# Opening of a linear-attention and gated-unit kernel: batch 0's second half of values and batch 1's edge planes issued later, batch 2's q and k ahead of the weights

## The chip, the cores and the metric

The kernel runs on one core of a Trainium2 chip. The metric is device time in microseconds (us) of one execution, smaller is better. The engines are TensorE (PE; PEld is its weight load), VectorE (DVE), ScalarE (ACT), GpSimd (POOL) and SyncE (SP, which only issues transfers and passes semaphores on). Transfers between device memory and the on-chip buffer (SBUF) are carried out by 16 DMA engines. GpSimd issues on queue q0, SyncE on q1, ScalarE on q10.

## What is computed

Hedgehog linear attention over 8 batches, 8 heads, 576 tokens, head dimension 64, followed by a causal gated linear unit. All inputs and the output are float32.

```python
def phi(x):
    proj = np.einsum('bhsd,df->bhsf', x, w_phi)              # 64 -> 128 features
    proj = proj - np.max(np.abs(proj), axis=-1, keepdims=True)
    return np.concatenate([np.exp(proj), np.exp(-proj)], axis=-1)
q_p, k_p = phi(q), phi(k)
kv  = np.einsum('bhsf,bhsd->bhfd', k_p, v);  z = np.sum(k_p, axis=2)
num = np.einsum('bhsf,bhfd->bhsd', q_p, kv)
den = np.einsum('bhsf,bhf->bhs', q_p, z)[..., None] + 1e-06
attn = num / den                                             # -> x: [8, 576, 512]
# second part, d_model 512
gate_pre[:, s] = sum over k of conv_w[k] * x[:, s - 4 + k]    # 5 causal taps
gate = 1 / (1 + exp(-gate_pre))
out  = (gate * (x @ w_val)) @ w_out
```

## The kernel before

Each batch is cut into 4 units, one for each pair of heads, and one smaller "edge" part. With x running over 128 partitions, a pair of heads has 9 token planes for each partition. Eight of them are worked on unit by unit, 32 units in all (0 to 3 are batch 0, 4 to 7 batch 1, and so on); the ninth plane of all four units of a batch together is the edge part (names that end in e, numbered by batch).

The order of all work is written out by hand in one string, `ORDER`, of some 1250 tokens. A token is an operation, the number of its unit or batch, after @ its PSUM banks, and after a colon the engine (P GpSimd, D VectorE, A ScalarE). The loop at the end calls `op_<name>` for each token in turn. Each engine runs its own instructions strictly in that order and waits at semaphores for the others. Where two tokens stand on different engines, their relative place in the string says nothing; where they share an engine or an issuing queue, it is the order.

The tokens that matter here, with the lines under which the profile shows them:

- Loads on GpSimd's queue (they turn float32 into bfloat16): `LQa LKa LKb LQb` are batch 0's q and k in pieces, `LQ1 LK1` and `LQ2 LK2` all of batch 1's and 2's (L287, tiles qN, kN); `LWV0` is w_val (L324, tile GV), `LWO0..3` quarters of w_out (L333, tile WOUT).
- Loads on SyncE's queue: `LVa` and `LVb` are the first and second half (two units each) of a batch's values, two transfers each (L292, tile vN); `LE` is its edge plane of values, two transfers in runs of 256 bytes (L297, tile vE).
- `T` transposes q and k of a unit on TensorE (L347), `Te` those of an edge (L637); `Tc` and `Tce` copy the result to SBUF (L154). `PK` and `PQA` project k and q to the features (L360), `mKa mKb mQ` take the maxima on VectorE (L377), `E` and `Ee` their exponentials (L426), `Ka Kb` the exponentials of k on ScalarE (L441), `KTe` those of the edge.
- `V` scales a unit's values on GpSimd (L467, L471; V0 and V1 read what LVa0 loads, V2 and V3 what LVb0 loads, V4 and V5 LVa1), `Ve` the edge's (Ve1 reads LE1). `KV` multiplies them with the k features (L488, L496).
- `PQa`, `PQb` project q a second time, transposed (L534), `DMQ` spreads the maxima on GpSimd (L412), `SH` subtracts them (L550), `Qp Qm` are the exponentials of q (L564).
- `WC` copies w_val, in a permuted layout, to tile WVAL on GpSimd (L154); the gated unit reads it from L839 on, and WOUT from L868 on. `TH` is the gate's tanh (L828).
- `WQ` is a relay: an empty instruction on SyncE (L526) that waits for the last matmul of `PQa`; the first matmul of `PQb` waits for the relay. SyncE's queue thus has transfers and relays in one order.

Lines of the loads and of the relay:

```python
def vload(b, j):
    vs = v[b].rearrange("h (p n) d -> p h (n d)", n=NPL)
    for a in range(2):
        nc.sync.dma_start(vals(b, j)[row(a), :, :], vs[:, 4 * j:4 * j + 4, 4 * a * D:(4 * a + 5) * D])
def op_LE(b):
    for g in range(2):
        e = 8 * D * (1 - g)
        nc.sync.dma_start(plane8(b)[:, g::2, :], src["v"][b, :, g::2, e:e + D])
def relay(u):
    u.relay = nc.sync.nop()
    behind(u.relay, u.last)
```

The buffers for q and k hold three batches, those for values four halves, those for edge planes two batches; so none of the loads of batches 0 to 2 named above waits for a buffer.

Of the kernel before, what the change touches and what calls it, by code (L numbers as in the profile page):

```python
# [20 lines left out]
P = 128  # L21
HP = H // 2
NPL = 9
E1 = D + 1
# [3 lines left out]
ORDER = """  # L28
ZV2:D ZV0:D IF0:D CQ0 CK0 LQa0 FL9@1 ND0:D ZV1:D LKa0 FL7@3 TP0@5 FL2@1 T0@2 CW0 W0 T1@1 Tc0:D PQA0@3 Tc1:A
mQ0 PK0@5,0 Ka0 PK1@6,7 mKb0 Kb1 FL1@2 LKb0 mKa1 LQb0 PQA1@1 mQ1 T2@3 mKa0 Te0@4 Tce0:D FL14@1 Kb0 Tc2:A  # L30
PQA2@0 PK2@4,5 LQ1 LK1 DG0:P LWV0 mKb1 Ka1 E0 E1 LWO0 LK2 LQ2 LE0 LVa0 PQa1@2 DMQ1:P LVb0 LE1 WQ1 DMQ0:P Kb2
V1:P mQ2 DMQ2:P Ka2 PKe0@6 mKe0 mKb2 PQb1 SH1 Ee0 KTe0 LWO1 T3@0 FL5@1 Tc3:D FL11@1 FL12@1 mKa2 FL13@1 Qm1 Qp1
PQa0@0 WQ0 PQb0 SH0 mQe0 PQa2@6 PQA3@4 WQ2 Qm0 PQb2 mQ3 DMQe0:P Ve0:P SH2 Qp0 Qp2 LWO3 V0:P T4@3 Tc4:D T6@2
PQA4@4 Qm2 LWO2 Tc6:D mQ4 DMQ4:P DMQ3:P Te1@3 PK4@1,2 Tce1:D mKa4 KV1@0 KVM1:D PQea0@4 LVa1 WQe0 Kb4 PKe1@6
# [988 lines left out]
```

## Time and profile before

| | |
|---|---|
| Three runs | 219.36, 221.36, 221.43 us; median 221.36 |
| The profiled execution | 220.76 us, of which 219.0 are the span from the first to the last instruction of the profile |
| Mean granted TensorE clock | 0.981 of full speed |
| Moved by the DMA engines | 32.40 MB, mean 148 GB/s |

A row of the timeline or of the chain begins with its start and its length in us, counted from the start of the span; then come engine, line, operation, tiles (out<-in), shapes, the number of instructions that were merged, and in brackets the idle time of that engine just before and what ended it. A row of waits reads "who <- for whom: us in total, times, longest". A row of issues ends with KB of each and median us from issue to landing. A queue row is packets, MB and the time of its packets as a share of 16 engines' time; with two queues at once such shares can add to more than 100%. A row of a stretch has its length, each engine's busy time and number of instructions, the granted clock, the DMA share and GB/s. SPq, POOLq are the issuing sides of these engines.

### The profile page before, as it was taken

To read this page: it belongs to the slowest core of one execution; us is meant where nothing else is said; L and a number is where in the kernel's file an instruction comes from. 1 tells how busy PE (TensorE), PEld (TensorE's weight loads), DVE (VectorE), ACT (ScalarE), POOL (GpSimd) and SP (SyncE) were. 2 spreads that over 40 slices of the span, in tenths; PEclk is the share of its full clock that TensorE was granted. 3 is DMA by queue.
4 is the path that set the end of the run, shared out by engine and by line. 5 is a ranking of instruction groups with operands and counts; after the bars stand their busy time and mean duration, and the time that the engine had idled before them with its cause. 6 is when DMAs were issued, how large, how long until landed. Compare 5 with 4: busy or idle time off the path is not lost.

```text
span 219.0 us, 8941 instructions
## 1 busy us (share of the span) xinstructions
PE 201.0 (92%) x3755; PEld 134.6 (61%) x3788; DVE 188.0 (86%) x339; ACT 193.7 (88%) x386; POOL 149.9 (68%) x180
## 2 busy tenths in 40 slices
PE   7676989979999999999999999999999999999991
PEld 2443758647676676766676668655576667656640
DVE  6786999989999999989989999898998999876362
ACT  3599899998999999999999999799999999988450
POOL 8969968999676498986864768595881695840000
PEclk9969699999999999999999999999999999999998
DMA  6999995069989912999980794719922800404726
GB/s 168 231 256 209 242 218 122 4 136 203 246 183 177 236 34 48 158 226 253 256 201 3 138 196 103 152 31 216 240 49 76 207 15 1 102 18 128 187 57 192
DMA packets 28194, 32.40 MB, mean 148 GB/s; under 512 B 6005, under 2 KB 23285, under 8 KB 28154
## 3 DMA queue, kind: packets, MB, share of 16 engines
q1 hardware_dynamic: 18282, 20.79, 38.7%
q0 software_dynamic: 9328, 10.19, 28.8%
q10 hardware_dynamic: 544, 0.85, 1.2%
q8 instruction: 29, 0.48, 0.9%
q14 instruction: 11, 0.09, 0.2%
HBM read 32.58 MB, written 9.44 MB: 192 GB/s over the span
## 4 chain that ended last, share of the span: by engine, by line
PE 67%; DMA 7%; POOL 6%; issue 5%; DVE 5%; ACT 4%; SPq 3%; POOLq 0%; DVEq 0%; ACTq 0%
PE PS L868 11%; PE PS L839 8%; DMA kN<-in_k_dram 7%; PE PS L496 7%; PE PS L582 6%; PE PS L347 5%; PE PS L360 5%; PE PS L612 4%; PE PS L534 4%; PE PS L796 3%; PE PS L550 3%; PE PS L488 2%; ACT KT L441 2%; PE PS L948 2%; POOL VT L467 2%
## 5 line engine op out<-in xcount | busy, mean ns | idle before, releaser
L467 POOL TENSOR_TENSOR VT<-vN,E 128x1024 bf16<-128x1024 f32 x32 | 61.0, 1905 | 23.3 <-ACT E L426 23.0
L441 ACT ACTIVATE KT<-PS 128x512 bf16<-128x512 f32 x128 | 69.2, 640 | 1.7 <-PE PS L360 0.9
L564 ACT ACTIVATE QT<-PS 128x1024 bf16<-128x1024 f32 x64 | 62.4, 1056 | 1.7 <-PE PS L550 1.4
L377 DVE TENSOR_REDUCE MK<-PS 128x4 f32<-128x512 f32 x64 | 42.6, 682 | 2.9 <-PE PS L360 2.2
L377 DVE TENSOR_REDUCE MQ<-PS 128x8 bf16<-128x1024 f32 x32 | 39.1, 1221 | 4.4 <-PE PS L360 3.8
L412 POOL TENSOR_TENSOR DM<-id,MQ 128x512 bf16<-128x512 bf16 x32 | 33.1, 1040 | 11.7 <-DVE MQ L377 11.4
L868 PE MATMUL PS<-WOUT,GV 128*128 128x512 bf16 x113 | 30.2, 379 | 1.2 <-issue 0.6
L839 PE MATMUL PS<-XT,WVAL 128*128 128x512 bf16 x115 | 29.9, 379 | 0.8 <-issue 0.2
L360 PE MATMUL PS<-W,T 64*128 64x128 bf16 x512 | 24.8, 222 | 2.1 <-ACT T L152 1.1
L496 PE MATMUL PS<-VT,KT 128*128 128x65 bf16 x512 | 24.0, 196 | 0.0
L860 DVE SCALAR_TENSOR_TENSOR GV<-GATE,PS 128x512 bf16<-128x512 bf16 x32 | 21.1, 682 | 3.4 <-ACT GATE L823 2.1
L360 PEld LDWEIGHTS <-T 64*128 64x128 bf16 x512 | 17.6, 97 | 9.1 <-issue 4.0
L602 DVE TENSOR_TENSOR XN<-PS,RCP 128x512 bf16<-128x512 f32 x32 | 21.9, 687 | 0.7
L496 PEld LDWEIGHTS <-KT 128*128 128x128 bf16 x512 | 21.7, 99 | 0.9
L582 PEld LDWEIGHTS <-QT 128*128 128x128 bf16 x512 | 18.4, 97 | 4.8 <-issue 2.4
L582 PE MATMUL PS<-KVS,QT 128*128 128x65 bf16 x512 | 20.8, 193 | 0.0
L534 PE MATMUL PS<-T,W 64*128 64x256 bf16 x128 | 17.8, 281 | 2.5 <-SPq L526 1.2
L154 DVE COPY T<-PS 128x1024 bf16<-128x1024 bf16 x27 | 18.2, 682 | 1.8 <-PE PS L347 1.8
L467 POOL TENSOR_TENSOR VZ<-vE,Ee 64x512 bf16<-64x512 f32 x16 | 16.6, 1039 | 2.9 <-ACT Ee L426 2.3
L839 PEld LDWEIGHTS <-WVAL 128*128 128x128 bf16 x128 | 11.2, 98 | 11.7 <-issue 0.9
L868 PEld LDWEIGHTS <-GV 128*128 128x128 bf16 x128 | 10.8, 98 | 10.8 <-issue 1.3
L488 PE MATMUL PS<-VZ,KTe 128*128 128x130 bf16 x64 | 14.3, 223 | 0.1
(92 smaller groups left out, 365.0 us busy)
## 6 DMA issues: line engine op xcount, KB each, us to landing
vN<-in_v_dram SPq DMA_DIRECT2D x32, 320.0 KB, 7.0
out_dram<-OS SPq DMA_DIRECT2D x28, 256.0 KB, 4.1
qN<-in_q_dram POOLq DMA_DIRECT2D x7, 576.0 KB, 11.4
kN<-in_k_dram POOLq DMA_DIRECT2D x7, 576.0 KB, 10.3
vE<-in_v_dram SPq DMA_DIRECT2D x16, 64.0 KB, 6.4
out_dram<-OSe SPq DMA_DIRECT2D x8, 128.0 KB, 4.8
GV<-in_moe_w_val_dram POOLq DMA_DIRECT2D x1, 512.0 KB, 16.0
WOUT<-in_moe_w_out_dram POOLq DMA_DIRECT2D x4, 128.0 KB, 13.6
```

Of the source, the lines that this page charges most:

```text
L360: (nc.tensor.matmul(PS[:, banks[g], jj * F:(jj + 1) * F], T[row(g), n, jj, :, :].rearrange("p a t -> p (a t)"), W2[row(g), :], start=True, ...
L377: nc.vector.tensor_reduce(dst, x, AX.X, ALU.max, apply_absolute_value=True)
L412: engines[eng].tensor_tensor(u.DM[:, :, :], id64[:, :].unsqueeze(1).to_broadcast([P, n, 64]), u.MQ[:, :, :].rearrange("p j g -> p (j g)"). ...
L441: nc.scalar.activation(u.KT[:, ft, par, :, :].rearrange("p b f -> p (b f)"), PS[:, u.PK[par], :], AF.Exp, scale=1.0 if ft == 0 else -1.0,)
L467: engines[eng].tensor_tensor(dst[:, :, :, 0:D].rearrange("p f (h m) d -> p f h m d", m=m), x.unsqueeze(1).to_broadcast(s), e.rearrange("p ...
L496: nc.tensor.matmul(o, u.KT[:, ft, y % 2, h2 * 2 + y // 2, :], u.VT[:, ft, h2 * 4 + y, :], start=False, stop=(y == 3), skip_group_check=True,)
L534: return nc.tensor.matmul(PS[:, u.PQ + a, :].rearrange("p (j g t) -> p g j t", g=2, t=64)[:, g, :, :], W2[row(g), :], u.T[row(g), 1, :, a, :],
L564: nc.scalar.activation(u.QT[:, ft, :, :, :].rearrange("p a n t -> p a (n t)"), half(u.PQ, 512), AF.Exp, scale=1.0 if ft == 0 else -1.0,)
L582: (nc.tensor.matmul(u.NUM[:, jj // 2, x * E1:(x + 1) * E1], u.QT[:, ft, jj // 2, 4 * h2 + 2 * (jj % 2):4 * h2 + 2 * (jj % 2) + 2, :].rearr ...
L602: nc.vector.tensor_tensor(u.XN[:, :, :, :], numview(u)[:, :, :, 0:D], u.RCP[:, :, :].unsqueeze(3).to_broadcast([P, 2, 4, D]), ALU.mult,)
L839: nc.tensor.matmul(PS[:, m.val[r], :], WVAL[:, dt, r, :], xt(b)[:, dt, 4:12, :].rearrange("p n t -> p (n t)"), start=(dt == 0), stop=(dt = ...
L868: nc.tensor.matmul(PS[:, m.out[j], :], m.GV[:, r, j * P:(j + 1) * P], WOUT[:, r, :], start=(r == 0), stop=(r == 3),)
```

## The change

Only the third line of `ORDER` differs:

```diff
-PQA2@0 PK2@4,5 LQ1 LK1 DG0:P LWV0 mKb1 Ka1 E0 E1 LWO0 LK2 LQ2 LE0 LVa0 PQa1@2 DMQ1:P LVb0 LE1 WQ1 DMQ0:P Kb2
+PQA2@0 PK2@4,5 LQ1 LK1 DG0:P mKb1 Ka1 E0 E1 LK2 LQ2 LWV0 LWO0 LE0 LVa0 PQa1@2 DMQ1:P WQ1 LVb0 LE1 DMQ0:P Kb2
```

On GpSimd's queue `LK2` and `LQ2` are issued ahead of `LWV0` and `LWO0` instead of behind them. On SyncE's queue `LVb0` and `LE1` stand behind the relay `WQ1` instead of ahead of it, so that they are issued after the last matmul of `PQa1`. No instruction is added or removed.

On SyncE (transfers with what each waits for; the relays themselves are not listed, a wait for PE is a relay's), at the second half of batch 0's values:

```order
 L292 DMA vN<-in_v_dram 64x4x320
 L292 DMA vN<-in_v_dram 64x4x320 [waits DMAHW0_49]
-L292 DMA vN<-in_v_dram 64x4x320 [waits DMAHW1_49]
+L292 DMA vN<-in_v_dram 64x4x320 [waits PE_49,DMAHW1_49]
 L292 DMA vN<-in_v_dram 64x4x320 [waits DMAHW2_49]
 L297 DMA vE<-in_v_dram 128x2x64 [waits DMAHW3_49]
```

The first of LVb0's two transfers now waits for TensorE; the rest of the row keeps its order.

On GpSimd, just before the first spreading of q's maxima (kN and qN here are batch 2's k and q, GV is w_val, WOUT the first quarter of w_out):

```order
 L278 TENSOR_TENSOR DIAG<-id_140,cwT 128x640
+L287 DMA kN<-in_k_dram 128x4x576
+L287 DMA qN<-in_q_dram 128x4x576
 L324 DMA GV<-in_moe_w_val_dram 128x4x512
 L333 DMA WOUT<-in_moe_w_out_dram 32x4x512
-L287 DMA kN<-in_k_dram 128x4x576
-L287 DMA qN<-in_q_dram 128x4x576
 L412 TENSOR_TENSOR DM<-id_138,MQ 128x512 x2
```

Batch 2's two loads have moved up past the two loads of weights.

## The prediction

> **What bounds the kernel now.** First the page: the engines' busy shares, and the shares of the chain of work that ended last.
>
> ```profile
> span 219.0 us, 8941 instructions
> PE 201.0 (92%) x3755; PEld 134.6 (61%) x3788; DVE 188.0 (86%) x339; ACT 193.7 (88%) x386; POOL 149.9 (68%) x180
> ...
> PE 67%; DMA 7%; POOL 6%; issue 5%; DVE 5%; ACT 4%; SPq 3%; POOLq 0%; DVEq 0%; ACTq 0%
> ```
>
> Taken over the whole span TensorE is the bound, with ScalarE and VectorE close behind. An average hides the opening, and the chain has 7% (15 us) in DMA. So next I read the chain in order of time over the first 48 us.
>
> ```profile
> 5.19 15.80 DMA kN<-in_k_dram
> 20.99 0.05 issue
> 21.03 0.63 PE PS L347 x8
> ```
>
> The transfer is LK1, batch 1's k: issued at 5.19, landed at 20.99, and then the transposes T4 and T6 (L347) run at once, the eight in 0.63. Third, the table of waits, from 19.5 to 45 us, for ScalarE, VectorE, GpSimd and TensorE.
>
> ```profile
> ACT KT L441 <- PE PS L360: 0.6, 1, 0.6
> ACT KT L441 <- DVE MK L377: 0.5, 1, 0.5
> ACT GATE L828 <- PE PS L796: 0.3, 1, 0.3
> ...
> DVE T L154 <- PE PS L347: 1.2, 1, 1.2
> ...
> POOL VT L467 <- ACT E L426: 1.2, 1, 1.2
> POOL VZ L467 <- ACT Ee L426: 1.1, 1, 1.1
> ...
> PE PS L347 <- DMA kN<-in_k_dram: 1.4, 1, 1.4
> ```
>
> LK1 costs TensorE 1.4 us and, behind it, VectorE 1.2. ScalarE has just three waits in 25 us: two hang on LK1's data, the third is that of the first tanh of batch 0's gate, far behind. GpSimd waits twice, both times for ScalarE. So after LK1 **ScalarE sets the pace**, and the change can be worth no more than what ScalarE waits behind LK1.
>
> **The change: when does LK1 land?** LK1 shares the DMA engines with SP's queue. The queue table over four stretches, in this order: 13 to 16 us, 28 to 30, 30.44 to 32.3, and 12.4 to 20.1.
>
> ```profile
> q0 software_dynamic: 331, 0.37, 70.3%
> q1 hardware_dynamic: 331, 0.40, 44.9%
> ...
> q0 software_dynamic: 354, 0.40, 117.5%
> ...
> q0 software_dynamic: 394, 0.37, 122.3%
> ...
> q0 software_dynamic: 942, 1.04, 78.2%
> ```
>
> q0 is GpSimd's queue, q1 SP's. With both full each moves 331 packets in 3 us, 110 per us, one for one. Alone, q0 moves 354 in 2 us: 177 per us. From 30.44 to 32.3 only q0 moves, although SP issued an LVb1 transfer at 30.44: a new transfer on SP's queue needs about 1.9 us to its first packet.
>
> Before, LVa0, LVb0 and LE1 are issued on SP in one run:
>
> ```profile
> 4.43 2.37 SPq L292 DMA_DIRECT2D vN<-in_v_dram  x3
> 6.84 1.24 SPq L297 DMA_DIRECT2D vE<-in_v_dram  x2
> ...
> vN<-in_v_dram SPq DMA_DIRECT2D x1, 320.0 KB, 9.2
> ```
>
> The 9.2 is that of the one issued at 4.43, LVa0's second piece: it lands at 13.6. How far does a landing trail its last packet? LVb1's second piece was issued at 31.1, and from 36 us on hardly a packet moves:
>
> ```profile
> 31.09 0.61 SPq L292 DMA_DIRECT2D vN<-in_v_dram  x1
> ...
> vN<-in_v_dram SPq DMA_DIRECT2D x1, 320.0 KB, 6.1
> ...
> 36.00:40.00 4.00, 3.96 (x88) 3.23 (x81) 4.00 (x11) 4.00 (x10) 3.99 (x5) 1.00 0.01 1
> ```
>
> (The last row is a stretch; its last two numbers are the DMA share and GB/s.) It landed at 37.2, about 1.2 later. So LVa0's packets end and LVb0's start at about 12.4, and from then on they and LE1's stand against LK1, whose own packets end at about 20.1, 0.9 before its landing. What q0 moved between, 942 packets, is the most that stood before LK1's end. After the change they wait for PQa1:
>
> ```profile
> 14.40 0.42 PE L534 MATMUL PS<-T,W 64*128 64x256 bf16 x2
> ```
>
> PQa1 ends at 14.82, so SP issues LVb0 at about 14.9, and its first packet goes at about 16.8. From 12.4 to 16.8 q0 is alone: 4.4 x 177 = 779 packets of its 942. The other 163 at 110 per us take 1.5 us: 18.3, and 0.9 to the landing gives **19.2 instead of 20.99**. From the other side: a restart after only 1.0 us leaves 322 packets to the shared rate, and 19.7.
>
> **What is late next.** T4 stands in TensorE's row behind SH2, Tc4 in VectorE's behind the maximum of unit 3's q:
>
> ```profile
> 19.27 0.38 PE L550 MATMUL PS<-DM,minus 64*128 64x512 bf16 x2
> ...
> 19.31 1.23 DVE L377 TENSOR_REDUCE MQ<-PS 128x8 bf16<-128x1024 f32 x1 [0.60 <-PE PS L360]
> 21.76 1.29 DVE L154 COPY T<-PS 128x1024 bf16<-128x1024 bf16 x2 [1.22 <-PE PS L347]
> ...
> 17.82 5.65 ACT L564 ACTIVATE QT<-PS 128x1024 bf16<-128x1024 f32 x6
> 24.05 2.18 ACT L441 ACTIVATE KT<-PS 128x512 bf16<-128x512 f32 x4 [0.58 <-PE PS L360]
> ...
> 27.94 1.09 ACT L441 ACTIVATE KT<-PS 128x512 bf16<-128x512 f32 x2 [0.54 <-DVE MK L377]
> ```
>
> SH2 ends at 19.65, so T4 runs then and, with the chain's 0.63, ends at 20.28. VectorE is busy to 20.54, and so Tc4 starts at 20.54 rather than 21.76: 1.22 gained, all of VectorE's wait. ScalarE's block of six q exponentials ends at 23.47 whatever LK1 does. PK4, whose end let ScalarE go at 24.05, comes 1.22 earlier, before 23.47: 0.58 gained. The second wait, at 27.94, ends with VectorE's maximum, which comes 1.22 earlier, at 26.7; ScalarE is then ready at 27.40 - 0.58 = 26.82, so this 0.54 goes too. Together **1.12 us**; then ScalarE has no wait up to that tanh, and GpSimd's two waits behind ScalarE, 1.2 and 1.1, take the shift up as well.
>
> **What the moves cost.** No transfer changes its place among SP's own; LVb0 and LE1 only come behind the relay of PQa1. That relay is not held up; those of PQa0 and PQa2 are now queued behind four issues. The relays of PQa1 and PQa0 passed at 14.9 and 17.7:
>
> ```profile
> L526 SPq EVENT_SEMAPHORE  x2: 17/17/17, 14.9 to 17.7; - x2
> ```
>
> By the issues above (2.37 for three vN is 0.79 each, 1.24 for two vE) the four take 2.8: SP is through at 17.7, when PQa0's relay passed. Cost between 0 and some tenths, and TensorE's wait for LK1 lies behind it; I take **0**.
>
> LVb0 feeds V2 on GpSimd, and the weights the WVAL copies there; the third row is Te2, the first to read batch 2's k:
>
> ```profile
> 26.98 1.90 POOL L467 TENSOR_TENSOR VT<-vN,E 128x1024 bf16<-128x1024 f32 x1
> ...
> 38.56 0.61 POOL L154 COPY WVAL<-GV 128x512 bf16<-128x512 bf16 x1
> ...
> 37.19 0.27 PE L637 MATMUL PS<-ident,kN 128*128 128x128 bf16 x2
> ```
>
> LVb0 is two pieces of 64x4 rows, 512 packets: from 16.8 at 110 per us to 21.5, landed by 23; V2, at 26.98, is held by GpSimd's own row before it. I take 0, with 4 us of cover.
>
> The Trainium skill, page "DMA: Bandwidth & Descriptors", section "Rules for kernel authors", speaks against this edit: issue a transfer early and wait for it late, so that its fixed cost lies under compute. By that rule alone, moving LVb0 ten microseconds later gains nothing, and the sum would be 0 or worse; by V2's row it is the sum below, and the case in which the rule wins is in the second rival.
>
> On GpSimd the same four issues stand before the same DMQ1, so it starts no later. All four stand behind LK1 on one queue, so LK1 does not feel the swap. By 36 us all of the opening's traffic was through (the stretch from 36 to 40, above). Batch 2's k and q, part of it, are first read at 37.19, so landing earlier buys nothing. The weights come later, but the order within the traffic does not change its amount. WVAL is read at 38.56, or 37.4 after the shift: 0, with over 1 us of cover in the worst case.
>
> **Sum:** -1.12, all in ScalarE's waits between 23 and 28 us. Everything later is released by engines, so I let it run to the end. The profiled execution: span 219.0, own time 220.76; it would be 217.9 and 219.65. The runs' median is 221.36, 0.6 above the profiled one, and gives 220.25. I forecast 220.0, between the two.
>
> **The rivals.**
>
> First, more than that: the shift also breaks a later wait. The next place where the chain is on SP is at 45 us:
>
> ```profile
> 45.75 2.04 SPq L297
> ...
> 48.42 0.28 PE L534 MATMUL PS<-T,W 64*128 64x256 bf16 x2 [1.23 <-SPq L526]
> ```
>
> One issue of LE2 there takes 2.04 us instead of 0.6, and TensorE waits 1.23 for the relay behind it. If it falls at a better moment, up to 1.2 more goes: 218.8. Against it: whatever slowed it shifts with it.
>
> Second, less: LK1 lands at 20 or later, or the gain is swallowed by GpSimd, which has no wait between 19.5 and V2's end (the table of waits: both of its waits are later ones).
>
> ```profile
> 32.64 0.22 PE PS L488
> ...
> vN<-in_v_dram SPq DMA_DIRECT2D x1, 320.0 KB, 13.1
> ```
>
> For it: 1.9 us for the restart rests on one case. Against: TensorE reads V2's result, complete at about 28.9, only at 32.64 (KV2, the first row). With half of T4's wait left it is -0.5, and 220.6. If LVb0's second piece took 13.1 us from its issue at 15.6, the longest that an early vN took, V2 would come at 28.7, 1.7 late; GpSimd's first wait (1.2) takes most of that, about 0.4 of the gain is left: 220.7. Nothing gained at all: 221.1.
>
> Third, slower: SP is not through in time. If both LE1 issues take 2.04 as at 45.75, SP is busy to 14.9 + 1.6 + 4.1 = 20.6, and the relay that passed at 17.7 is 2.9 late. TensorE's wait for LK1 takes 1.4 of it; 1.5 is left as loss, 222.6, and more if the relay behind it finds TensorE waiting again. It decides from about 19.1 on. Against it: the five early issues in the rows above took 3.6 us together, 0.72 each.
>
> **How the numbers follow.** Forecast 0.5; more 0.18; less or nothing 0.22; slower 0.10. The three runs lie 2.07 apart, so each case spreads by about 1 around its time; 1% is 2.2 us (219.15 and 223.57), about what a measurement of this kernel tells from no change. Faster by over 1%: 0.12 from the first rival, 0.09 from the forecast's lower edge and 0.02 from the second: 0.23. Slower by over 1%: half of the third, where later relays are late too, 0.05. Within: 0.72. The range runs from the first rival less some spread, 218.4, to the third's near edge, 222.0.
>
> **What would show it.** Right: the row of T4 no longer names kN as what it waited for; Tc4 starts near 20.5; ScalarE has no wait from 17.8 to beyond 40; V2 still starts near 27; the first WVAL copy comes about 1.1 earlier, near 37.4; the granted clock of 0.50 between 24 and 26 us may be gone, which would shorten matmuls there but not the time, since ScalarE sets the pace. Wrong: a wait of V2 for vN, of the WVAL copy for GV, of L534 on SP at 17.8 to 20, or a wait that appears after 40 us and gives the 1.1 back.

## The result, and the profile after

The change makes the kernel faster, by 0.5 to 1.2%. Three measurements on the chip, each beside runs of the kernel before. The ratio is over the executions outside the chip's slower state and is not the quotient of the two medians:

| | runs | median us | before, median us | ratio, 95% interval |
|---|---|---|---|---|
| first | 19 | 218.88 | 220.62 (19 runs) | 0.9946 (0.9924 to 0.9967) |
| second | 6 | 218.42 | 220.62 (23) | 0.9884 (0.9835 to 0.9932) |
| third | 12 | 219.04 | 220.51 (23) | 0.9929 (0.9895 to 0.9962) |

In all three the interval lies below 1. The profiled execution took 219.53 us with a span of 217.7 (before: 220.76 and 219.0). The table of waits of ScalarE in the changed kernel, from 17.5 to 45 us:

```profile
ACT GATE L828 <- PE PS L796: 0.3, 1, 0.3
```

Of before's three waits only that of the first tanh is left. TensorE's largest waits from 17.5 to 22 us:

```profile
PE PS L534 <- DVE MQe L377: 0.6, 1, 0.6
PE PS L360 <- DVE T L154: 0.4, 1, 0.4
PE PS L347 <- ACT QT L564: 0.2, 1, 0.2
```

The 1.4 for kN is gone; what holds L347 now is ScalarE, for 0.2. The issue of LK1 (queue table, KB and us from issue to landing) and SyncE's row:

```profile
kN<-in_k_dram POOLq DMA_DIRECT2D x1, 576.0 KB, 13.9
...
15.06 1.26 SPq L292 DMA_DIRECT2D vN<-in_v_dram  x2
16.36 1.12 SPq L297 DMA_DIRECT2D vE<-in_v_dram  x2
```

LK1 lands 13.9 us after its issue at 5.04, at 18.9, where it took 15.8 before. ScalarE's row, at its six exponentials of q, the two places that waited, and the first tanh:

```profile
18.42 5.68 ACT L564 ACTIVATE QT<-PS 128x1024 bf16<-128x1024 f32 x6
23.84 2.22 ACT L441 ACTIVATE KT<-PS 128x512 bf16<-128x512 f32 x4
...
25.94 1.27 ACT L722 ACTIVATE QTe<-PS 128x512 bf16<-128x512 f32 x2
26.89 1.30 ACT L441 ACTIVATE KT<-PS 128x512 bf16<-128x512 f32 x2
...
40.96 1.94 ACT L828 ACTIVATE GATE<-PS 128x1024 bf16<-128x1024 f32 x2 [0.29 <-PE PS L796]
```

No bracket stands at 23.84 and 26.89, where before had 0.58 and 0.54. The same places of before (the block at 17.82, the exponentials at 24.05 and 27.94 stand in the prediction):

```profile
26.31 1.08 ACT L722 ACTIVATE QTe<-PS 128x512 bf16<-128x512 f32 x2
...
41.79 1.02 ACT L828 ACTIVATE GATE<-PS 128x1024 bf16<-128x1024 f32 x1 [0.28 <-PE PS L796]
```

This cuts both executions into three pieces, which is how all the runs below are compared: the **opening** up to the first exponential of q, the **stretch** from there to the first tanh of the gate, and the **rest**.

| | opening | stretch | rest | span |
|---|---|---|---|---|
| before | 17.82 | 23.97 | 177.2 | 219.0 |
| changed | 18.42 | 22.54 | 176.8 | 217.7 |

The opening is 0.6 longer, the stretch, where the change acts, 1.43 shorter, and the rest 0.4 shorter. Further profiles, below, show how far each of the three moves by chance.

### The profile page after: what moved, and what is told of

It is laid out like the page before. It is cut to its first block, busy times and chain, and to the rows that moved or that the text cites. A ratio compares the mean times of both kernels' runs of the same rounds, so it can differ in the third digit from the quotient of the medians.

```text
span 217.7 us, 8974 instructions
## 1 busy us (share of the span) xinstructions
PE 203.6 (94%) x3788; PEld 134.1 (62%) x3788; DVE 187.7 (86%) x339; ACT 192.9 (89%) x386; POOL 149.6 (69%) x180
## 4 chain that ended last, share of the span: by engine, by line
PE 77%; ACT 13%; DMA 3%; issue 3%; DVE 3%; POOL 1%; POOLq 0%; SPq 0%; ACTq 0%; DVEq 0%
PE PS L868 13%; PE PS L839 12%; PE PS L582 7%; PE PS L496 7%; PE PS L360 6%; ACT KT L441 6%; PE PS L347 6%; PE PS L534 4%; PE PS L796 4%; ACT QT L564 4%; PE PS L612 4%; PE PS L550 3%; DMA kN<-in_k_dram 3%; PE PS L488 2%; PE PS L948 2%
## 5 line engine op out<-in xcount | busy, mean ns | idle before, releaser
L868 PE MATMUL PS<-WOUT,GV 128*128 128x512 bf16 x128 | 32.2, 380 | 0.0
L839 PE MATMUL PS<-XT,WVAL 128*128 128x512 bf16 x128 | 31.3, 379 | 0.0
L496 PEld LDWEIGHTS <-KT 128*128 128x128 bf16 x512 | 21.2, 98 | 1.7 <-issue 0.7
## 6 DMA issues: line engine op xcount, KB each, us to landing
WOUT<-in_moe_w_out_dram POOLq DMA_DIRECT2D x4, 128.0 KB, 15.9
```

The source lines that it names most:

```text
L496: nc.tensor.matmul(o, u.KT[:, ft, y % 2, h2 * 2 + y // 2, :], u.VT[:, ft, h2 * 4 + y, :], start=False, stop=(y == 3), skip_group_check=True,)
L839: nc.tensor.matmul(PS[:, m.val[r], :], WVAL[:, dt, r, :], xt(b)[:, dt, 4:12, :].rearrange("p n t -> p (n t)"), start=(dt == 0), stop=(dt = ...
L868: nc.tensor.matmul(PS[:, m.out[j], :], m.GV[:, r, j * P:(j + 1) * P], WOUT[:, r, :], start=(r == 0), stop=(r == 3),)
```

## The experiments

The theory at this point, called A in the expectations: SyncE's part is all of the change; it lets LK1 land earlier, and ScalarE loses its waits behind LK1. Rival B: batch 2's q and k ahead of the weights carry a share. Rival C: the difference between the two profiles is chance, above all the slow issue of LE2 with the relay behind it at 48 us.

### Either part alone

SyncE's part alone:

```diff
-... LE0 LVa0 PQa1@2 DMQ1:P LVb0 LE1 WQ1 DMQ0:P Kb2
+... LE0 LVa0 PQa1@2 DMQ1:P WQ1 LVb0 LE1 DMQ0:P Kb2
```

> SyncE's part alone: LVb0 and LE1 behind the relay WQ1, GpSimd's row as before. Theory A (SyncE's part is all of it: LK1 lands earlier and ScalarE loses its two waits of 0.58 and 0.54): LK1 lands 13.5 to 14.5 us after its issue instead of 15.8, ScalarE has no wait between its block of q exponentials and the first tanh of the gate, ratio to before 0.993 to 0.997, as the whole change (0.9946). Theory B (batch 2's q and k ahead of the weights carry a share): about half of the gain, 0.997 to 0.999. Theory C (the gain of the profiled pair is the relay wait of 1.23 us at 48 us, a matter of chance): ratio spread around 0.995 with or without ScalarE's waits, and the profile shows which of the two issues of LE2 was slow.

GpSimd's part alone:

```diff
-... DG0:P LWV0 mKb1 Ka1 E0 E1 LWO0 LK2 LQ2 LE0 ...
+... DG0:P mKb1 Ka1 E0 E1 LK2 LQ2 LWV0 LWO0 LE0 ...
```

> GpSimd's part alone: LK2 and LQ2 ahead of LWV0 and LWO0, SyncE's row as before. Theory A: LK1 lands 15.8 us after its issue as before, TensorE waits about 1.4 us for kN and ScalarE 0.5 to 0.6 twice; ratio 0.998 to 1.002. Theory B: 0.997 to 0.999, with LK1 landing as before and a wait gone behind it. Theory C: any ratio within 0.993 to 1.002, by LE2's issue.

SyncE's part: 218.09 us median of 6, ratio 0.9875 (0.9828 to 0.9922). GpSimd's part: 220.50 of 12, ratio 0.9993 (0.9955 to 1.0032). The issue of LK1 and the two ends of the stretch, first SyncE's part, then GpSimd's:

```profile
kN<-in_k_dram POOLq DMA_DIRECT2D x1, 576.0 KB, 13.5
...
17.23 5.65 ACT L564 ACTIVATE QT<-PS 128x1024 bf16<-128x1024 f32 x6
39.74 1.94 ACT L828 ACTIVATE GATE<-PS 128x1024 bf16<-128x1024 f32 x2 [0.28 <-PE PS L796]
```

```profile
kN<-in_k_dram POOLq DMA_DIRECT2D x1, 576.0 KB, 16.1
...
18.76 5.72 ACT L564 ACTIVATE QT<-PS 128x1024 bf16<-128x1024 f32 x6
41.38 1.94 ACT L828 ACTIVATE GATE<-PS 128x1024 bf16<-128x1024 f32 x2 [0.28 <-PE PS L796]
...
PE PS L347 <- DMA kN<-in_k_dram: 0.6, 1, 0.6
```

SyncE's part alone has LK1 early and a stretch of 22.51. Its ratio lies below the 0.993 to 0.997 that A expected, but the whole change, measured beside the same runs of before, came to 0.9884 (next section): the part is worth as much as the whole, and B is refuted as far as the time goes. GpSimd's part leaves LK1 where it was, as A says. But its stretch is 22.62, not 24: a miss of A's expectation in the profile (two waits of ScalarE were expected, there is none). The opening of this execution was long, 18.76, and LK1's landing came just 2.4 us behind the first exponential of q, where before had 3.2. A late opening hides LK1.

### Both kernels once more

> The kernel before once more, unchanged, with a profile of its own: what differs from the first profile is chance. Theory A: ratio 1.000 within 0.003; LK1 lands 15 to 16.5 us after its issue, TensorE's wait for kN is 1.0 to 1.8, ScalarE's two waits are there. Theory C: the slow issue of LE2 (2.04 us) is gone or elsewhere, and the span differs by about 1.2.

> The changed kernel once more, unchanged, with a profile of its own. Theory A: ratio 0.992 to 0.997; LK1 lands 13 to 14.5 us after its issue, no wait of TensorE for kN, none of ScalarE up to the tanh. Theory C: LE2's issue may be slow here, with a wait of 1.2 for the relay behind it and a span of about 218.9; the two stalls of 0.4 among the taps' matmuls (65 and 73 us in the first profile) come or stay away by chance.

The unchanged kernel before: 221.07 of 12, ratio 1.0014 (0.9982 to 1.0047). The changed one: 0.9884, above. ScalarE's waits and the ends of the stretch of the kernel before:

```profile
ACT KT L441 <- PE PS L360: 1.1, 1, 1.1
ACT KT L441 <- DVE MK L377: 0.6, 1, 0.6
...
17.37 5.73 ACT L564 ACTIVATE QT<-PS 128x1024 bf16<-128x1024 f32 x6
41.92 1.02 ACT L828 ACTIVATE GATE<-PS 128x1024 bf16<-128x1024 f32 x1 [0.29 <-PE PS L796]
```

and the changed kernel's ends:

```profile
19.48 5.66 ACT L564 ACTIVATE QT<-PS 128x1024 bf16<-128x1024 f32 x6
42.01 1.02 ACT L828 ACTIVATE GATE<-PS 128x1024 bf16<-128x1024 f32 x1 [0.28 <-PE PS L796]
```

Before: opening 17.37, stretch 24.55. The first wait is longer than in the first profile; the opening was shorter, and TensorE's half clock, of which more below, set in 0.4 earlier. Changed: opening 19.48, stretch 22.53; its ratio missed A's 0.992 to 0.997 on the good side. C's slow issue of LE2 at 45.75 was not in this second profile of before, nor in any other profile of this case: it is chance, and so not what made the changed kernel faster on average. The stalls among the taps' matmuls, which C named, are chance too. TensorE's waits from 60 to 80 us of the kernel before (where its first profile had none above 0.3):

```profile
PE PS L796 <- issue: 1.1, 1, 1.1
PE PS L923 <- issue: 0.7, 1, 0.7
```

### Which of the two transfers

LE1 alone behind the relay, then LVb0 alone:

```diff
-... DMQ1:P WQ1 LVb0 LE1 DMQ0:P Kb2
+... DMQ1:P LVb0 WQ1 LE1 DMQ0:P Kb2
```

> As the changed kernel, but LVb0 back ahead of the relay WQ1 and only LE1 behind it. Theory A counts packets: in SyncE's queue LE1 stands behind LVb0, whose 512 packets last to about 17 us at 110 per us, and LE1 is issued at 15; so the queue never runs dry and nothing changes against the kernel before: LK1 lands 15.3 to 16.3 us after its issue, TensorE waits for kN unless the opening is late. Theory D (what counts is how many bytes are moved later, LE1 being a sixth of them): LK1 lands 0.3 to 0.4 us earlier than before.

```diff
-... DMQ1:P WQ1 LVb0 LE1 DMQ0:P Kb2
+... DMQ1:P LE1 WQ1 LVb0 DMQ0:P Kb2
```

> As the changed kernel, but LE1 ahead of the relay WQ1 and only LVb0 behind it. Theory A: LE1's 512 small packets go from 12.4 one for one with LK1's at about 148 per us each, until 15.9; then SyncE's queue is dry for about 1 us until LVb0's first packet at 16.8. LK1 lands 14.2 to 15.0 us after its issue, between the changed kernel (13.9) and the one before (15.8). Theory D (bytes): five sixths of the gain, 14.0 to 14.2.

LK1's issue and TensorE's wait with LE1 alone behind the relay, then LK1's issue with LVb0 alone behind it:

```profile
kN<-in_k_dram POOLq DMA_DIRECT2D x1, 576.0 KB, 16.1
PE PS L347 <- DMA kN<-in_k_dram: 1.2, 1, 1.2
```

```profile
kN<-in_k_dram POOLq DMA_DIRECT2D x1, 576.0 KB, 14.4
```

Each has a single execution (220.51 and 219.39 us), so the profiles decide, not the times. LE1 alone leaves LK1 as late as before (stretch 23.22, for a reason told below); LVb0 alone gives the whole of the stretch (22.54). D, the count of bytes, had LE1 alone at 0.3 to 0.4 us, which is missed. LVb0 alone does not tell the two theories apart: its 14.4 lies 0.2 from D's range, and the changed kernel's own profiles have 13.5 to 14.3. What does is the queue table of the kernel before from 18 to 20 us, where LE1's runs of 256 bytes go beside LK1's packets:

```profile
q0 software_dynamic: 297, 0.32, 92.9%
q1 hardware_dynamic: 296, 0.07, 29.0%
```

Packet for packet, though q0 moves more than four times the bytes. And LE1 behind LVb0 in the same queue is no competitor until LVb0 is through.

### One relay later

```diff
-... DMQ1:P WQ1 LVb0 LE1 DMQ0:P Kb2 ... PQa0@0 WQ0 PQb0 SH0 ...
+... DMQ1:P WQ1 DMQ0:P Kb2 ... PQa0@0 WQ0 LVb0 LE1 PQb0 SH0 ...
```

> As the changed kernel, but LVb0 and LE1 one relay later, behind WQ0 (about 17.7 us) instead of WQ1. Theory A: LK1 lands 13.0 to 13.5 us after its issue, earlier than in the changed kernel, and no relay stands behind an issue of LE1; but ScalarE has no wait there to give, so the time is that of the changed kernel: ratio to before 0.987 to 0.996, from ScalarE's first q exponential to the first tanh the same 22.5 us as there. V2 still starts without waiting for vN. Theory E (earlier is better, LK1 still bounds): ratio below 0.987, and the stretch from q exponential to tanh shorter.

Ratio 0.9964 (0.9925 to 1.0003), 10 runs. LK1's issue, SyncE's row and TensorE's:

```profile
kN<-in_k_dram POOLq DMA_DIRECT2D x1, 576.0 KB, 13.9
...
18.27 1.25 SPq L292 DMA_DIRECT2D vN<-in_v_dram  x2
19.57 1.12 SPq L297 DMA_DIRECT2D vE<-in_v_dram  x2
...
20.80 0.28 PE L534 MATMUL PS<-T,W 64*128 64x256 bf16 x2 [0.98 <-SPq L526]
```

Three misses. LK1 does not land earlier than in the changed kernel (13.9 as there): in the changed kernel LVb0 already came too late to meet it. And the statement that no relay stands behind an issue of LE1 was wrong: the relay of PQa2 does, TensorE waits 0.98 for it with T4 queued behind. So the stretch is 23.28 instead of 22.5, and the ratio lies just outside the 0.987 to 0.996 that was expected. This is the prediction's third rival, seen at work: from its place one relay later, SyncE's row is what is late.

### Another order of the opening

LVa0 leaves SyncE's queue for GpSimd's, between batch 0's and batch 1's loads:

```diff
-... LQ1 LK1 DG0:P ... LWO0 LE0 LVa0 PQa1@2 ...
+... LVa0 LQ1 LK1 DG0:P ... LWO0 LE0 PQa1@2 ...
-            nc.sync.dma_start(vals(b, j) ...
+            (nc.gpsimd if b + j == 0 else nc.sync).dma_start(vals(b, j) ...
```

> As the changed kernel, and LVa0 too leaves SyncE's queue: it is issued on GpSimd's, between batch 0's and batch 1's q and k, so that in the first 15 us q0 carries everything in the order in which it is needed, with only LE0 beside it. Theory A: what is left in the opening is ScalarE's path, and that begins with batch 0's own loads; with LVa0 out of their way LQb0 lands at 9.5 to 10.5 instead of 12.0 to 12.6 us, ScalarE's first q exponential starts 0.5 to 1.5 earlier than in the changed kernel's runs, LK1 lands at 17.5 to 19, and the ratio to before is 0.981 to 0.991. Theory F (the opening hangs on the first k piece, LKa0, at 7 to 9 us, and on the clock): first q exponential as before within 0.3, ratio as the changed kernel's.

Ratio 0.995 (0.9915 to 0.9985), 12 runs, median 219.06: no better than the change. In the profile batch 0's last q did land earlier, 6.77 us after its issue at 3.60, and the opening was 16.90; but LK1, now behind LVa0 in GpSimd's queue and issued at 6.36, landed at 19.6, past the 17.5 to 19 that was expected:

```profile
16.90 5.73 ACT L564 ACTIVATE QT<-PS 128x1024 bf16<-128x1024 f32 x6
...
19.68 0.40 PE L347 MATMUL PS<-ident,kN 128*128 128x128 bf16 x4 [0.87 <-DMA kN<-in_k_dram]
...
39.83 1.94 ACT L828 ACTIVATE GATE<-PS 128x1024 bf16<-128x1024 f32 x2 [0.29 <-PE PS L796]
```

What the opening gained, the stretch (22.93) partly gave back. The ratio expected, 0.981 to 0.991, was missed.

### A third measurement, and the relays kept free

> The changed kernel a third time, against the kernel before on the same chip as the next run. Theory A: ratio 0.987 to 0.996, between or at the two earlier results (0.9946 and 0.9884); 22.5 us from the first q exponential to the first tanh, whatever the opening before it takes; the opening itself (first q exponential between 17.2 and 19.5 so far) now goes into the time in full. Theory E (LK1 still bounds at times): the stretch is longer than 22.7 in this run.

```diff
-... DMQ1:P WQ1 LVb0 LE1 DMQ0:P Kb2 ... PQA3@4 WQ2 Qm0 ...
+... DMQ1:P WQ1 LVb0 DMQ0:P Kb2 ... PQA3@4 WQ2 LE1 Qm0 ...
```

> As the changed kernel, but LE1 two relays later, behind WQ2, so that no relay of PQa0 or PQa2 stands behind four issues on SyncE: after LVb0's two they find the queue free. Theory A: LK1 lands as in the changed kernel (13.4 to 14.4 us after its issue), no TensorE wait for a relay before 22 us, LE1 lands by 30, ahead of its reader at about 32; first q exponential to first tanh 22.5, since the relays' delay (0.84 once, none otherwise) was covered by ScalarE's row: ratio as the run beside it within 0.003. Theory G (late relays cost the changed kernel something in many executions): 0.003 or more below it.

Both gave 0.9929 (0.9895 to 0.9962, and 0.9897 to 0.9960; 12 runs each, medians 219.04 and 218.58). Keeping the relays free changes nothing that can be measured: nothing speaks for G, but with intervals of 0.003 to either side a cost of the size that G had is not excluded. In the profile with LE1 behind WQ2, LVb0 was issued already at 13.9, LK1 took 14.9, more than A's 13.4 to 14.4, and TensorE waited 0.8 for it; the stretch was 22.79.

### All profiles in one table

"Lag" is from the first exponential of q to the landing of LK1.

| kernel | LK1, us from issue | lag | stretch |
|---|---|---|---|
| before, second profile | 15.9 | 3.5 | 24.55 |
| before | 15.8 | 3.2 | 23.97 |
| LE1 alone | 16.1 | 3.0 | 23.22 |
| LVa0 on GpSimd's queue | 13.3 | 2.7 | 22.93 |
| LE1 behind WQ2 | 14.9 | 2.6 | 22.79 |
| GpSimd's part alone | 16.1 | 2.4 | 22.62 |
| LVb0 alone | 14.4 | 1.7 | 22.54 |
| changed, third profile | 13.5 | 1.3 | 22.53 |
| SyncE's part alone | 13.5 | 1.3 | 22.51 |
| changed | 13.9 | 0.5 | 22.54 |
| changed, second profile | 14.3 | 0.1 | 22.53 |

(The kernel with the late relay, 23.28 at a lag of 0.6, is held by SyncE and left out.) The stretch has a floor of 22.5 us, nearly all ScalarE's own work (22.25 busy in the changed kernel), and rises once LK1 lands more than about 2.4 us behind the first exponential of q. That is the mechanism, shown in eleven profiles. It does not hold all of the two rows of before: from a lag of 2.4 to 3.0 the stretch grows by 0.6, as much as the lag, but from 3.0 to 3.5 by 1.3. What else they hold is told under "The granted clock".

## Why the prediction was right

The way was as forecast: LVb0 later, LK1 earlier, ScalarE's waits gone, nothing lost elsewhere. That the forecast gain of 1.12 lies near the 1.23 of the two profiled executions (220.76 and 219.53) is in part luck, as the terms below show. The time of 220.0 against 218.88 is off mostly by its base: the three runs had a median of 221.36, 19 runs of the same kernel 220.62.

**LK1's landing.** Forecast 19.2, measured 18.9, but by another route than the working. LVb0's restart was taken at 1.9 us. The queue table of the changed kernel from 15.06, LVb0's issue, to 18.9:

```profile
q0 software_dynamic: 698, 0.78, 118.9%
q8 instruction: 1, 0.02, 1.6%
```

No packet of q1 in 3.8 us: the restart took twice the estimate, and LK1, through by then, did not meet LVb0 at all. In the traces of all eight profiles with LVb0 behind a relay its first packet went 3.9 us after its issue. Against that LVa0 came later than in the execution of before (its second piece landed at 14.2 instead of 13.6), so q0 was alone later. q0's rate alone, 698 packets in 3.84 us, is 182 per us, where 177 was used. The errors partly cancel, so a landing within 0.3 is partly luck.

**What is late next.** T4 waits for ScalarE instead of kN, VectorE's and ScalarE's waits are gone, as forecast. The term of the sum was mis-sized: 1.12 was forecast, 1.43 measured in the stretch. The idle time in brackets understates a wait on ScalarE, since its instructions overlap: in the changed kernel the block of six q exponentials ends at 24.10 (18.42 + 5.68), but the next exponential starts at 23.84. From the block's start to the next exponentials of k it was 6.23 (17.82 to 24.05) before and 5.42 (18.42 to 23.84) after: 0.81, where the bracket said 0.58. From QTe to the second place it was 1.63 (26.31 to 27.94) and 0.95 (25.94 to 26.89): 0.68, where it said 0.54. These two are where the 1.43 was lost; not all of it was lost to LK1, as the next paragraph shows.

**The granted clock.** The sentence that the half clock in 24 to 26 us costs no time was wrong. The rows of before, with TensorE at 0.50 of full speed, and of LE1 alone, from 22.8 to 26.2 us:

```profile
22.80:26.20 3.40, 3.40 (x54) 2.81 (x52) 2.98 (x6) 2.81 (x6) 3.39 (x5) 0.50 1.17 247
```

```profile
22.80:26.20 3.40, 2.90 (x60) 2.14 (x61) 3.40 (x6) 2.98 (x6) 3.34 (x4) 1.00 1.16 242
```

LE1 alone has LK1 as late as before: T4 starts at 21.31, where before has 21.03. Its T4, its eight matmuls of PK4 and its first tanh, then PK4's eight in before:

```profile
21.31 0.40 PE L347 MATMUL PS<-ident,kN 128*128 128x128 bf16 x4 [1.21 <-DMA kN<-in_k_dram]
23.44 0.40 PE L360 MATMUL PS<-W,T 64*128 64x128 bf16 x8
...
41.48 1.94 ACT L828 ACTIVATE GATE<-PS 128x1024 bf16<-128x1024 f32 x2 [0.29 <-PE PS L796]
```

```profile
23.38 0.61 PE L360 MATMUL PS<-W,T 64*128 64x128 bf16 x8
```

Six profiles have a T4 that waits for LK1, and from its start to the first tanh the work is the same in all:

| kernel | T4 starts | first tanh | between | clock of 0.50 between |
|---|---|---|---|---|
| before, second profile | 20.95 | 41.92 | 20.97 | 22.4 to 25.8 |
| before | 21.03 | 41.79 | 20.76 | 22.8 to 26.2 |
| LE1 alone | 21.31 | 41.48 | 20.17 | none |
| LVa0 on GpSimd's queue | 19.68 | 39.83 | 20.15 | none |
| LE1 behind WQ2 | 19.96 | 40.12 | 20.16 | none |
| GpSimd's part alone | 21.23 | 41.38 | 20.15 | none |

At full clock it is 20.16 whatever the lag; the half clock added 0.6 and 0.8. So of the 1.43 that the profiled pair gained in the stretch, 0.83 was LK1's lateness (T4 at 3.21 behind the block's start, and 20.16, make 23.37 against 22.54) and about 0.6 the half clock. The forecast laid its whole 1.12 to LK1, which is too much for LK1 alone, and put the clock at nothing. Whether LK1's lateness also brings the half clock about is open: it came in the two profiles with the longest waits for LK1 (1.7 and 1.4 us), and in none of those with 1.2 or less. On average the gain is not only the clock's: among the executions on record with a mean granted clock of 0.990 or more, 29 of before take 220.3 us in the mean and 17 of the changed kernel 218.8. (A mean of 0.990 still has room for one such dip, which is 0.8% of the span.) No run changed the clock alone.

**What the moves cost.** Nothing, as forecast. V2 started in GpSimd's row without a wait, the WVAL copies as well; rows of the changed kernel:

```profile
27.60 1.90 POOL L467 TENSOR_TENSOR VT<-vN,E 128x1024 bf16<-128x1024 f32 x1
...
37.72 0.61 POOL L154 COPY WVAL<-GV 128x512 bf16<-128x512 bf16 x1
```

The rule of the Trainium skill that was weighed there, "DMA: Bandwidth & Descriptors", section "Rules for kernel authors", to issue early and wait late, is not refuted but has its limit here: an early transfer also took packets from one that was needed sooner, which the measured 15.8 against 13.9 us of LK1 shows.

**The sum.** "Everything later is released by engines, so I let it run to the end" was right on average and wrong for a single pair. In the pair of profiles the changed kernel lost 0.6 in the opening, which the forecast had not foreseen. Over the changed kernel's three profiles the opening came out between 17.2 and 19.5; three against two of before cannot tell whether the change has a part in that. While LVb0 is early, LK1 lands at about 21 (20.9 to 21.3 with openings from 17.4 to 18.8: both profiles of before, GpSimd's part alone, LE1 alone); the changed kernel has no such cover and passes a long opening on to the end. After the stretch, single events of up to 1.3 us (a slow issue ahead of a relay, stalls among the taps' matmuls) come and go by chance in both kernels. The three ratios, 0.988 to 0.995, do not contradict one another: their intervals share 0.9924 to 0.9932.

**The rivals.** More: no; LE2's slow issue was chance, present in one of the profiles. Less: happens in executions with a long opening (GpSimd's part alone shows how a lag of 2.4 hides LK1 without the change). Slower: not with this change. Its mechanism was seen with SyncE's part alone, where TensorE waited for the relay of PQa0 but ScalarE's row covered it:

```profile
PE PS L534 <- SPq L526: 0.8, 1, 0.8
```

and one relay later, where it cost.

## What to carry to other kernels

Where transfers on two queues share the DMA engines, count packets, not bytes: what is not needed soon takes turns with what is needed now, and a transfer behind another in its own queue competes only from where that one ends. Put such a transfer behind an event just late enough, and check what else stands in the queue of the engine that issues it: one relay further, the issues themselves became the wait. Judge such a change by the stretch in which it acts, from one instruction to another on the engine that sets the pace, since a single span carries chance of the size of the gain.

## What the runs showed of the hardware

A transfer issued on SyncE's queue while GpSimd's queue was full had no packet in the next 3.8 us (changed kernel), where one of before had none in 1.9; the wait from issue to first packet is not a constant, and why it differs is not shown. And an engine's idle time before an instruction can be a quarter shorter than what the wait costs (0.58 against 0.81, 0.54 against 0.68), because ScalarE's instructions overlap their neighbours when they do not wait. The Trainium skill, page "ScalarE: Activation LUTs", section "What ACT_TABLE_LOAD costs", gives about 93 ns for the overlap of two back to back; the trace has more here, 24.10 - 23.84 = 0.26 us at the end of the block. TensorE at half clock for 3.4 us cost the kernel 0.6 to 0.8 us, although ScalarE was the engine that set the pace: behind LK1, ScalarE waited for TensorE's matmuls and for VectorE's maxima of their results.
